# First batch row of a threshold attention + MLP-mixer kernel: three score slots in one PSUM tile, another rate of weight conversion, and the square on ScalarE

## Chip, cores, metric

One Trainium2 chip, one core. The metric is device time in microseconds (us) of one execution. Each kernel was executed several times; an execution is called a run here. The profile of the kernel before was taken on a further execution.

## The reference, cut

```python
# q, k, v: (8, 8, 576, 64) float32; tau = 0.02
scores = (q @ k^T) / 8
scores = where(scores >= rowmax(scores) - tau, scores, -1e9)
attn = softmax(scores)
x = (attn @ v), heads side by side          # (8, 576, 512)
# MLP mixer, weights in float64:
h = relu(x^T @ w_tok1) @ w_tok2             # 576 -> 256 -> 576, along the tokens
u = x + h^T
out = u + relu(u @ w_ch1) @ w_ch2           # 512 -> 1536 -> 512, along the channels
```

## The kernel before

The eight batch entries ("batch rows") are worked on in 144 units, 18 per row; a unit is 128 query rows of two heads. A unit's scores are computed at step u, its maximum, threshold and exponential in the same step, its transposes and products with v two or more steps later. From row 1 on, the MLP matmuls of the row before are strewn between the units by a quota (`fill`). The float64 weights are turned into float32 on the chip, in 31 pieces of three steps each; these 93 steps are spread over the units of rows 0 and 1 (`weight`), and a step that an MLP matmul needs is pulled forward (`need`).

The kernel uses eight PSUM banks. Two tiles of two banks hold scores, two banks hold transposes and products with v, two hold MLP results.

```python
ps_sc = ctx.enter_context(tc.tile_pool(name="ps_sc", bufs=2, space=bass.MemoryType.PSUM))
ps_tr = ctx.enter_context(tc.tile_pool(name="ps_tr", bufs=2, space=bass.MemoryType.PSUM))
ps_mm = ctx.enter_context(tc.tile_pool(name="ps_mm", bufs=2, space=bass.MemoryType.PSUM))
ctx.enter_context(tc.manual_schedule())
# ... cut ...
def f64_to_f32(dst, raw, rows, n):                         # one piece, three steps
    # ... cut: lo, hi = the two 32-bit words; a, h2 = scratch, h2 has ONE buffer ...
    nc.scalar.activation(out=lo.bitcast(I32), in_=lo, func=AF.Copy, scale=2.0**-29)
    nc.gpsimd.tensor_tensor(out=h2, in0=hi.bitcast(F32), in1=hi.bitcast(F32), op=ALU.mult)
    yield nc.vector.tensor_scalar(out=a, in0=hi, ...)      # shift, mask
    yield nc.vector.scalar_tensor_tensor(out=a, in0=hi, ...)   # OR: sign
    nc.vector.scalar_tensor_tensor(out=af, in0=h2, scalar=2.0**-30, in1=af, op0=ALU.is_ge, op1=ALU.mult)
    nc.gpsimd.tensor_tensor(out=dst..., in0=a..., in1=lo..., op=ALU.add)
# ... cut ...
def scores(u):
    b, p0, t = units[u]
    sc = [ps_sc.tile([P, 2, MAIN], F32, tag="sc", name=f"sc{h}_{u}") for h in range(2)]
    # ... cut ...
    for f in range(2):
        for n, cols, rows in parts:
            qT, kT = heads[n]
            for h in range(2):
                r = slice(D * h, D * h + D)
                nc.tensor.matmul(sc[h][rows, f, 0:HS], lhsT=qT[r, cols], rhs=kT[r, HS * f : HS * f + HS], start=True, stop=True)
    # ... cut ...
        nc.vector.tensor_reduce(out=mx[:, c], in_=sc[h][:, :, 0:HS], axis=AX.XY, op=ALU.max)
        nc.gpsimd.tensor_scalar(out=bias[:, c], in0=mx[:, c], ...)
def weigh(u):
    # ... cut ...
        nc.scalar.activation(out=eh, in_=sc[h][:, :, 0:HS], func=AF.Prelu, bias=bias[:, h : h + 1], ...)   # last reader of sc
    # ... cut: Exp in place ...
# ... cut; of the channel MLP:
def ch1(j):
    need(7 + j)
    ps = ps_mm.tile([P, GR], F32, tag="mm", name=f"c1_{b}_{i}_{j}")[:, 0:n]
    for c in range(NCC):
        nc.tensor.matmul(ps, lhsT=wc1[:, j, c, :], rhs=uT[:, c, GR * i : GR * i + n], start=(c == 0), stop=(c == NCC - 1))
    nc.scalar.activation(out=s["g"][:, j, 0:n], in_=ps, func=AF.Relu)
# ... cut; the main loop, per unit:
    scores(u)                       # if any are left
    norm(u - 1)                     # then transposes of unit u - 2
    if b_now: fill(0.4)
    weight(2)
    weigh(u)
    if b_now: fill(0.3)
    # ... products with v that are due ...
    if b_now: fill(0.3)
    weight(1 if b_now == 0 else 3)
```

## Time and profile before

| | before |
|---|---|
| time, median of 3 runs | 1425.71 us (1424.91 to 1426.79) |
| granted TensorE clock, mean | 0.982 |
| first maximum of unit 0 / 18 / 26 / 36 / 143 | 10.7 / 122.0 / 198.9 / 287.4 / 1222.0 us |
| row 0 (unit 0 to 18) | 111.3 us |
| stretch in which the conversion ends (unit 18 to 26) | 76.9 us |
| unit 26 to 143 | 1023.1 us |

The third row is read from the starts of VectorE's `tensor_reduce` in the trace. First the list of waits over the whole run (waiter, releaser: us in total, times, longest):

```profile
DVE mx L286 <- PE sc L281: 490.1, 125, 10.4
...
ACT g L447 <- PE c L446: 361.6, 160, 27.8
```

These are waits of engines that have less to do than TensorE, each for its own data: the maximum for its scores, the relu for its sum. They cost nothing by themselves.

### The profile page before, as it was taken

Reading aid. Unit: us, or ns where it says so; the run is one execution under the profiler, and the core shown is the slowest. Engines: PE = TensorE matmul, PEld = TensorE weight load, DVE = VectorE, ACT = ScalarE, POOL = GpSimd, SP = SyncE. Lnnn points to the kernel's source line nnn. Section 1 sums busy time; section 2 is a strip of 40 time slices with the busy share of each in tenths; the row PEclk is TensorE's granted clock in tenths of the full one; section 3 lists DMA queues with packets and bytes.
Section 4 is the critical chain, followed back from the end, with each engine's and each line's share of the span. In section 5 each row is a group of like instructions: output and inputs, shape, how many; then the busy total and the mean of one; then the engine's idle time right before and its main releaser. Section 6 shows DMA issues by size and latency. Waiting matters only on the chain.

```text
span 1425.1 us, 19472 instructions
## 1 busy us (share of the span) xinstructions
PE 1350.8 (95%) x6866; PEld 833.5 (58%) x6866; DVE 584.2 (41%) x1000; ACT 575.5 (40%) x1306; POOL 380.9 (27%) x712
## 2 busy tenths in 40 slices
PE   5866899978999999999999999999999999999998
PEld 3543475644756466565656566566657466566675
DVE  5778764344444443434433444434333444201000
ACT  4665453443544444353334444443333444220110
POOL 4777652221222222222212222222121222100000
PEclk9898899989999999999999999999999999999999
DMA  5444544443444434433343434443433433300000
GB/s 123 118 110 126 142 124 98 95 116 81 96 120 112 108 84 109 107 93 79 95 99 77 120 83 111 99 102 72 103 84 85 110 89 80 81 17 15 8 8 23
DMA packets 257376, 128.34 MB, mean 90 GB/s; under 512 B 208064, under 2 KB 221376, under 8 KB 257280
## 3 DMA queue, kind: packets, MB, share of 16 engines
q1 hardware_dynamic: 134000, 111.75, 30.0%
q10 hardware_dynamic: 123280, 15.35, 6.8%
q8 instruction: 55, 0.90, 0.3%
q14 instruction: 41, 0.34, 0.1%
HBM read 43.25 MB, written 9.44 MB: 37 GB/s over the span
## 4 chain that ended last, share of the span: by engine, by line
PE 82%; DVE 5%; SPq 4%; POOL 3%; ACT 2%; DMA 2%; issue 1%; DVEq 0%; POOLq 0%
PE c L462 26%; PE c L446 24%; PE sc L281 10%; PE pv L388 7%; PE t L417 4%; SPq L353 4%; PE t L424 3%; PE pv L383 2%; DVE T L343 2%; PE tx L407 1%; DVE mx L286 1%; PE c L458 1%; DMA eT<-T 1%; PE tr L332 1%; POOL scratch L156 1%
## 5 line engine op out<-in xcount | busy, mean ns | idle before, releaser
L446 PE MATMUL c<-xT,wc 128*128 128x256 f32 (+1 forms) x1920 | 405.5, 363 | 1.3 <-DVE xT L428 0.8
L286 DVE TENSOR_REDUCE mx<-sc 128x1 f32<-128x576 f32 x288 | 204.5, 751 | 490.1 <-PE sc L281 490.1
L462 PE MATMUL c<-wc,g 128*128 128x512 f32 x864 | 389.5, 597 | 0.0
L446 PEld LDWEIGHTS c<-xT,wc 128*128 128x128 f32 x1920 | 331.1, 190 | 74.7 <-issue 29.5
L287 POOL TENSOR_SCALAR bias<-mx,toff 128x1 f32<-128x1 f32 x288 | 76.0, 265 | 795.0 <-DVE mx L286 744.1
L296 ACT ACTIVATE e<-sc,bias 128x576 f32<-128x576 f32 x288 | 198.6, 738 | 179.0 <-POOL bias L287 167.2
L462 PEld LDWEIGHTS c<-wc,g 128*128 128x128 f32 x864 | 157.6, 190 | 177.3 <-issue 176.1
L447 ACT ACTIVATE g<-c 128x256 f32<-128x256 f32 (+1 forms) x240 | 86.8, 362 | 391.1 <-PE c L446 361.6
L299 ACT ACTIVATE e<-e,ntau 128x576 f32<-128x576 f32 x288 | 220.2, 773 | 0.0
L281 PE MATMUL sc<-kT,qT 64*128 64x288 f32 (+1 forms) x1280 | 197.4, 442 | 23.7 <-ACT e L296 15.1
L309 POOL TENSOR_SCALAR e<-e,rr 128x576 f32<-128x576 f32 x288 | 213.5, 754 | 16.3 <-DVE rr L306 4.0
L343 DVE STREAM_TRANSPOSE T<-e 128x1152 f32<-128x1152 f32 x126 | 172.5, 1369 | 17.2 <-DMA eT<-T 12.7
L281 PEld LDWEIGHTS sc<-kT,qT 64*128 64x128 f32 (+1 forms) x1280 | 107.1, 182 | 108.2 <-issue 49.5
L388 PE MATMUL pv<-eT,lv 128*64 128x256 f32 x1024 | 128.6, 396 | 0.0
L467 DVE COPY o<-c 128x512 f32<-128x512 f32 x36 | 24.6, 684 | 192.3 <-PE c L462 192.3
L388 PEld LDWEIGHTS pv<-eT,lv 128*64 128x64 f32 x1024 | 77.5, 143 | 39.9 <-issue 4.9
L424 PE MATMUL t<-w,a 128*128 128x288 f32 x256 | 76.1, 426 | 11.6 <-DVE xT L428 9.8
L417 PE MATMUL t<-x,w 128*128 128x512 f32 (+1 forms) x160 | 77.2, 621 | 0.0
L393 ACT COPY xT<-pv 128x256 f32<-128x256 f32 x64 | 23.8, 372 | 113.6 <-PE pv L388 113.3
L428 DVE TENSOR_TENSOR xT<-xT,t 128x288 f32<-128x288 f32 x64 | 27.9, 441 | 95.8 <-PE t L424 95.7
L424 PEld LDWEIGHTS t<-w,a 128*128 128x128 f32 x256 | 45.4, 191 | 35.3 <-DVE xT L428 14.7
L299 ACT ACTIVATION_READ_ACCUMULATOR e<-e,ntau 128x1 f32 x288 | 57.1, 198 | 0.0
(43 smaller groups left out, 621.8 us busy)
## 6 DMA issues: line engine op xcount, KB each, us to landing
eT<-T SPq DMA_DIRECT2D x896, 72.0 KB, 2.1
scratch<-in_moe_w_ch_dram SPq DMA_DIRECT2D x24, 512.0 KB, 3.7
lv<-in_v_dram SPq DMA_DIRECT2D x32, 288.0 KB, 3.4
out_dram<-o SPq DMA_DIRECT2D x36, 256.0 KB, 2.1
eT<-T SPq DMA_DIRECT2D x224, 36.0 KB, 1.9
lq<-in_q_dram ACTq DMA_DIRECT2D x104, 72.0 KB, 2.2
lk<-in_k_dram ACTq DMA_DIRECT2D x104, 72.0 KB, 2.7
lq<-in_q_dram SPq DMA_DIRECT2D x24, 72.0 KB, 3.4
```

Source lines behind the costliest of these rows:

```text
L281: nc.tensor.matmul(sc[h][rows, f, 0:HS], lhsT=qT[r, cols], rhs=kT[r, HS * f : HS * f + HS], start=True, stop=True)
L286: nc.vector.tensor_reduce(out=mx[:, c], in_=sc[h][:, :, 0:HS], axis=AX.XY, op=ALU.max)
L296: nc.scalar.activation(out=eh, in_=sc[h][:, :, 0:HS], func=AF.Prelu, bias=bias[:, h : h + 1], scale=SCALE, alpha=STEEP)
L299: nc.scalar.activation(out=eh, in_=eh, func=AF.Exp, bias=ntau, accum_out=rs[:, h : h + 1])
L309: nc.gpsimd.tensor_scalar(out=eh, in0=eh, scalar1=rr[:, h : h + 1], scalar2=1.0, op0=ALU.mult, op1=ALU.mult)
L343: nc.vector.transpose(out=T.rearrange("p (a c n x) -> p c a n x", a=4, c=NK, n=n)[:, :, :, place, :], in_=e.rearrange("p (c a x) -> p c a ...
L388: nc.tensor.matmul(to[r], lhsT=lv[:, j, :], rhs=eT[:, j], start=False, stop=(c == NI - 1), skip_group_check=True)
L417: nc.tensor.matmul(ps, lhsT=w1[0:M, t, P * m : P * m + P], rhs=s["x"][0:M, t, :], start=(t == 0), stop=(t == NT - 1))
L424: nc.tensor.matmul(ps, lhsT=s["a"][:, m, P * c : P * c + P], rhs=w2[:, m, HS * f : HS * f + HS], start=(m == 0), stop=(m == NTK - 1))
L446: nc.tensor.matmul(ps, lhsT=wc1[:, j, c, :], rhs=uT[:, c, GR * i : GR * i + n], start=(c == 0), stop=(c == NCC - 1))
L447: nc.scalar.activation(out=s["g"][:, j, 0:n], in_=ps, func=AF.Relu)
L462: nc.tensor.matmul(flat, lhsT=s["g"][:, j, P * t : P * t + P], rhs=wc2[:, j, :], start=False, stop=(j == NJ - 1), skip_group_check=True)
```

## The change

Intent: give row 0, where no engine is full, a third score slot, by using in row 0 the two banks that the MLP needs only from row 1 on; do fewer conversion steps in row 0 and more in row 1 (three a unit become two, five become seven); take the square off GpSimd; share the middle transposes' copies between ScalarE and VectorE; load the first q and k from two queues. To let two banks serve both purposes, the six banks become one tile, of which slices are handed out. The core of the diff:

```diff
-    ps_sc = ctx.enter_context(tc.tile_pool(name="ps_sc", bufs=2, space=bass.MemoryType.PSUM))
+    ps_big = ctx.enter_context(tc.tile_pool(name="ps_big", bufs=1, space=bass.MemoryType.PSUM))
     ps_tr = ...
-    ps_mm = ctx.enter_context(tc.tile_pool(name="ps_mm", bufs=2, space=bass.MemoryType.PSUM))
+    banks = ps_big.tile([P, 6, MAIN], F32, name="banks")
+    mm_last, mm_held = [0], [None]
+    def mm_bank(hold=False):
+        i = mm_last[0] ^ 1
+        if i == mm_held[0]:
+            i ^= 1
+        mm_last[0] = i
+        if hold:
+            mm_held[0] = i
+        return banks[:, 4 + i, :]
@@ f64_to_f32
-        nc.gpsimd.tensor_tensor(out=h2, in0=hi.bitcast(F32), in1=hi.bitcast(F32), op=ALU.mult)
+        nc.scalar.activation(out=h2, in_=hi.bitcast(F32), func=AF.Square)
@@ first loads of q and k
-    load_qk(0, nc.sync)
+    load_qk(0, (nc.sync, nc.scalar))
@@ scores
-        sc = [ps_sc.tile([P, 2, MAIN], F32, tag="sc", name=f"sc{h}_{u}") for h in range(2)]
+        at = [h if b else (2 * u + h) % 3 for h in range(2)]
+        sc = [banks[:, 2 * a : 2 * a + 2, 0:HS] for a in at]
-        for f in range(2): ... for n, cols, rows in parts: ... for h in range(2): ...
+        order = [(f, part, h) for f in range(2) for part in parts for h in range(2)]
+        for f, (n, cols, rows), h in order if b else sorted(order, key=lambda o: o[2]):
@@ turn
-        on = nc.scalar.copy if third == 1 else nc.vector.tensor_copy
+        on = nc.scalar.copy if third == 1 and u % 2 else nc.vector.tensor_copy
@@ tok1, tok2, ch1, ch2: ps_mm.tile(...) becomes mm_bank(); ch2 holds its bank until its last part
@@ main loop
-        weight(2)
+        weight(4 if b_now else 1)
-        weight(1 if b_now == 0 else 3)
+        weight(3 if b_now else 1)
```

More of the change, by code (lines that the diff above doesn't have):

```diff
@@ L100, in load_qk @@
             h, c = divmod(i, 2)
-            for src, t in zip((q, k), loaded[n]):
-                eng.dma_start(
+            for src, t, on in zip((q, k), loaded[n], eng):
+                on.dma_start(
                     out=t[32 * i : 32 * i + 32], in_=src[b, 2 * p + h, :, 32 * c : 32 * c + 32].rearrange("(n t) d -> t n d", t=32)
@@ L224 @@
     load_piece(0)
-    load_qk(1, nc.sync)
+    load_qk(1, (nc.sync, nc.sync))
     load_v(0)
@@ L275, in scores @@
             parts = [(b * NP + p0 + i, slice(P * c, P * c + P), slice(0, P))]
-        for f in range(2):
-            for n, cols, rows in parts:
-                qT, kT = heads[n]
-                for h in range(2):
-                    r = slice(D * h, D * h + D)
-                    nc.tensor.matmul(sc[h][rows, f, 0:HS], lhsT=qT[r, cols], rhs=kT[r, HS * f : HS * f + HS], start=True, stop=True)
+        order = [(f, part, h) for f in range(2) for part in parts for h in range(2)]
+        for f, (n, cols, rows), h in order if b else sorted(order, key=lambda o: o[2]):
+            r = slice(D * h, D * h + D)
+            qT, kT = heads[n]
+            nc.tensor.matmul(sc[h][rows, f, :], lhsT=qT[r, cols], rhs=kT[r, HS * f : HS * f + HS], start=True, stop=True)
         mx = small.tile([P, 2], F32, tag="mx", name=f"mx_{u}")
@@ L285, in scores @@
             c = slice(h, h + 1)
-            nc.vector.tensor_reduce(out=mx[:, c], in_=sc[h][:, :, 0:HS], axis=AX.XY, op=ALU.max)
+            nc.vector.tensor_reduce(out=mx[:, c], in_=sc[h], axis=AX.XY, op=ALU.max)
             nc.gpsimd.tensor_scalar(out=bias[:, c], in0=mx[:, c], scalar1=toff, scalar2=-SCALE, op0=ALU.add, op1=ALU.mult)
@@ L295, in weigh @@
             eh = e[:, S * h : S * h + S].rearrange("p (f x) -> p f x", f=2)
-            nc.scalar.activation(out=eh, in_=sc[h][:, :, 0:HS], func=AF.Prelu, bias=bias[:, h : h + 1], scale=SCALE, alpha=STEEP)
+            nc.scalar.activation(out=eh, in_=sc[h], func=AF.Prelu, bias=bias[:, h : h + 1], scale=SCALE, alpha=STEEP)
         for h in range(2):
@@ L413, in tok1 @@
                 s["a"] = work.tile([P, NTK, DM], F32, tag="a", bufs=1, name=f"a_{b}")
-            ps = ps_mm.tile([P, DM], F32, tag="mm", name=f"t1_{b}_{m}")
+            ps = mm_bank()
             for t in range(NT):
@@ L421, in tok2 @@
             need(6)
-            ps = ps_mm.tile([P, HS], F32, tag="mm", name=f"t2_{b}_{c}_{f}")
+            ps = mm_bank()[:, 0:HS]
             for m in range(NTK):
@@ L443, in ch1 @@
                 s["g"] = work.tile([P, NJ, GR], F32, tag="g", bufs=1, name=f"g_{b}_{i}")
-            ps = ps_mm.tile([P, GR], F32, tag="mm", name=f"c1_{b}_{i}_{j}")[:, 0:n]
+            ps = mm_bank()[:, 0:n]
             for c in range(NCC):
@@ L452, in ch2 @@
             if part == 0:
-                s["ps"] = ps_mm.tile([P, NCC, P], F32, tag="mm", name=f"c2_{b}_{i}_{t}")
+                s["ps"] = mm_bank(hold=True).rearrange("q (c d) -> q c d", c=NCC)
             ps = s["ps"]
@@ L465, in ch2 @@
             if part == 3:
+                mm_held[0] = None
                 o = work.tile([P, DM], F32, tag="o", name=f"o_{b}_{i}_{t}")
@@ L551 @@
             if t < 8 and m < len(pairs):
-                load_qk(m, nc.scalar if b_now else nc.sync, t % 4)
+                load_qk(m, (nc.scalar if b_now else nc.sync,) * 2, t % 4)
                 if t % 4 == 3:
```

## The prediction

> **What bounds the kernel now.** I read the page first: over the whole span TensorE is the bound.
>
> ```profile
> PE 1350.8 (95%) x6866; PEld 833.5 (58%) x6866; DVE 584.2 (41%) x1000; ACT 575.5 (40%) x1306; POOL 380.9 (27%) x712
> PE   5866899978999999999999999999999999999998
> DVE  5778764344444443434433444434333444201000
> ```
>
> The reader sees that TensorE is at 9 in nearly every slice except the first ten or so. The change touches only the beginning, so I then asked for busy time by stretch. The cuts are the first score matmul (8.4), the first maximum of batch row 1, which is unit 18 (122.0), and the end of the weight conversion (199).
>
> ```profile
> 8.40:122.00 113.60, 84.63 (x518) 51.80 (x518) 84.80 (x164) 70.98 (x153) 79.85 (x113) 0.92 0.49 119
> 122.00:199.00 77.00, 61.98 (x304) 39.02 (x305) 60.92 (x95) 38.98 (x82) 52.31 (x63) 0.90 0.50 135
> 199.00:1425.00 1226.00, 1204.15 (x6045) 742.70 (x6044) 436.27 (x737) 464.29 (x1071) 247.43 (x527) 0.99 0.35 84
> ```
>
> Columns: stretch, length, then busy time of PE, weight load, VectorE, ScalarE, GpSimd, then clock, DMA share, GB/s. Batch row 0 (18 units in 113.6 us) has no engine above 75%: it runs on a loop of waits. After 199 us, TensorE idles 22 us of 1226, so what row 0 gains arrives at the end one for one, and nothing else can. The ceiling on what a perfect row 0 could give is small against 1425.
>
> The waits of 8 to 123 us show the loop.
>
> ```profile
> ACT eT L334 <- PE tr L332: 24.5, 17, 2.3
> PEld sc L281 <- ACT e L296: 18.5, 18, 4.2
> DVE scratch L163 <- POOL scratch L156: 14.7, 15, 1.5
> PE sc L281 <- ACT e L296: 11.9, 8, 3.3
> DVE mx L286 <- PE sc L281: 9.1, 9, 2.4
> ```
>
> Columns: waiter, releaser, total us, times, longest. Three things to see. The next unit's scores wait for Prelu of this unit, because two score buffers hold exactly one unit; Prelu stands in ScalarE's queue behind the copy of the middle transposes, which waits for TensorE: a ring of 5.9 us per unit in the first 45 us. VectorE waits 14.7 us for the square on GpSimd. Later in row 0 the period is 5.7 us in units without value matmuls and 6.3 to 7.6 with them; the mean is (122.0 - 10.7)/18 = 6.18 us.
>
> **What the Trainium skill says.**
> "ScalarE: Activation LUTs", section "What ACT_TABLE_LOAD costs": an ACTIVATE with immediates takes 186 ns + 0.833 ns per element, the same for every function; a switch of table set costs 1283 ns plus a drain. The trace agrees: the conversion's existing Copy of 128x512 takes 683 ns in row 0 (the formula gives 613; its source has a stride), and the one table load took 1283 ns. The section "Table sets" says cheap functions are in every set; it names relu, copy, identity and abs, not Square, so that Square needs no load is my assumption. No run shows it yet.
> "GPSIMD Engine Reference", section "Key points": GpSimd shares its SBUF interfaces with VectorE, in contention with VectorE instructions that have two SBUF inputs. The trace agrees: the two-input OR of the conversion (128x512) took 0.69 us alone, 1.10 us on average in row 0, and 1.66 at worst.
> "TensorE: Matmul & The Clock Gate", section "The mechanism": matmuls in different row groups overlap. The trace agrees: at 107.67 and 107.68 us the matmuls of the two heads start together, and the eight records of a unit end within 1.24 us though each lasts 0.40. The same page, section "What's actually happening", has an idle TensorE at half clock; here a score record lasts 0.68 us in the cold stretches and 0.40 in the warm ones.
>
> **The change part by part.**
>
> *Start.* The first q and k tiles are issued from two queues. Eight issues at about 0.53 us each on one queue (0.73 to 5.0 us) become four on each, behind the tau load on ScalarE's. The last issue moves from 4.5 to about 2.8 to 3.2 us, the first transposes and score matmul (8.41) follow. Estimate: **-1.7 us**.
>
> *Three score slots.* In row 0 head h of unit u waits for the Prelu three heads back, not two, so TensorE need not wait for Prelu of the unit just before. The 18.5 us wait and the ring above go.
>
> *Scores head by head.* Sorting by head puts matmuls of one row group one after the other. Starts in one row group are 0.24 us apart in the warm state, so eight take about 8 x 0.24 + 0.2 = 2.1 us instead of 1.24; the first head is ready after about 1.1 us, as before, and the second by the time VectorE has done the first maximum (0.75 us). So it costs TensorE 0.9 us a unit, and little latency.
>
> *Conversion steps.* 18 units x 3 steps = 54 steps (18 pieces) become 36 (12 pieces). VectorE loses 6 pieces x (0.46 + 1.10 + 0.69) = 13.5 us. The square moves to ScalarE: GpSimd loses 1.4 us a piece, ScalarE gains about 0.65, and VectorE's 14.7 us of waiting goes, since the square now comes a step or more ahead of its use.
>
> *Copies.* Nine of 18 middle copies go from ScalarE to VectorE, 9 x 0.54 = 4.9 us.
>
> Load per unit of row 0 after:
> - VectorE: two maxima 1.42 (back to back), norm 0.45, copies 2.5 x 0.5 = 1.27, conversion 2/3 x 2.0 = 1.34, transposes of q and k 0.34: **4.8 us** (before, 4.7 busy and 1.6 waiting).
> - ScalarE: Prelu and Exp 3.3, half a copy 0.24, conversion 2/3 x 1.33 = 0.9, value copies 0.25: **4.7 us**.
> - TensorE, warm: scores 2.1, transposes 1.3, values 1.34 on average: **4.7 us**, and more when cold.
> - GpSimd: bias 0.53, norm 1.5, conversion 0.85, the rest 0.15: 3.0 us, from 4.4.
>
> Three engines at 4.7 to 4.8 us cannot interleave perfectly. In the units with four large value groups per nine, the ring is: maxima 1.42, norm 0.45, first eT copy 0.54 (it frees a transpose bank), value matmuls 2.55, first head's scores 1.1, and in half of them the last transposes 0.65 before the values: 6.1 to 6.7, mean 6.4 us. The four units without values run at VectorE's 4.8; the one with small value groups at about 5. Mean (4 x 6.4 + 4 x 4.8 + 5)/9 = 5.5 us, against 6.18: 18 x 0.65 = **-11.5 us**. I take off 1.5 us for the first five units, where TensorE is cold and serial scores double in length too: **-10 us**.
>
> *Row 1.* 57 steps (19 pieces) are left for row 1 instead of 39 (13), at 7 per unit instead of 5, so conversion still ends in its ninth unit, and no later step is pulled forward. VectorE in these units: before 60.9 busy and some 8 waiting for GpSimd, of 77.0. After: 6 more pieces x 2.1 = +12.6, less contention with GpSimd on the other 13, about -4, the 7.2 us of waiting gone: about 70 of 77, so the stretch is close to VectorE-bound. ScalarE gets 19 squares (+12.4) and 6 copies (+4.1), about 56 busy. Its square now waits in order for VectorE to have used the previous one (one buffer), with Prelu behind it. Estimate: **+1 us**, with a wide spread (-3 to +8).
>
> *After row 1.* The matmuls, buffers (two banks, one skipped while held) and quotas are as before: 0.
>
> Sum: -1.7 - 10 + 1 = -10.7, so **1415.0 us**.
>
> **The rivals.**
> *A. Row 0 becomes engine-bound and nothing else.* If the three slots decouple the engines well, row 0 runs at 4.9 us a unit: 18 x 1.28 = -23, with the start -25: about 1401. For it: three loads are equal at 4.8. Against it: the order on each queue is fixed, TensorE has value matmuls in front of the next scores, and two transpose banks remain.
> *B. The gain is given back in row 1.* VectorE and ScalarE together have 29 us more in the 77 us where they already stalled TensorE (15 us idle there). If Prelu behind the squares holds up the scores and the relus that free the two MLP banks, 1 us a unit more is lost: 1421 to 1424. For it: the old trace has up to 5.6 us of ScalarE waiting for bias in that stretch. Against it: the removed GpSimd square was itself a cause.
> *C. Serial scores on a cold TensorE eat the gain.* At half clock, scores take about 4.1 us and transposes 2.4, 6.5 us a unit, no better than 6.18. If half of row 0 is cold, the row saves about 5 us: 1420. For it: 10 us stretches at half clock are seen in the old row 0 (the slice at 60 to 70 us has 0.55). Against it: a busier TensorE should be cold less.
> *D. Square needs its own table.* Then two loads per piece, 31 x 2 x 1.28 = 80 us on ScalarE, and the time goes above 1460. It is unlikely.
>
> **Range and chances.** B and C together give about 1424, A gives 1401; the range is 1402 to 1424. Faster by 2% means below 1397.2, more than rival A gives: 0.03. Slower by 2% needs D: 0.02. Within 2%: 0.95.
>
> **What would show each step.** In the profile after: first score matmul near 6.7 us; unit 18's first maximum near 110 us (122.0 before), that is 5.6 us a unit; no wait of VectorE's last conversion step on GpSimd; score records in row 0 of one head after the other, 2.1 us per unit when warm; no further table load; conversion ending about 77 us after unit 18; TensorE's idle time after that near 22 us as before. I would be wrong if row 0 takes under 92 or over 108 us for its 18 units, if the stretch from unit 18 to the end of conversion grows by more than 8 us, or if anything after it differs by more than 3 us.

## More of the kernel before

TensorE's timeline somewhere in the middle (start, length, line, count):

```profile
240.30 1.20 PE L281 MATMUL sc<-kT,qT 64*64 64x288 f32 x16
241.43 7.17 PE L446 MATMUL c<-xT,wc 128*128 128x256 f32 x32
248.53 1.24 PE L281 MATMUL sc<-kT,qT 64*128 64x288 f32 x8
```

Scores, 32 MLP records (four groups of eight) and the next unit's scores follow each other with no gap.

Second, the view of one source line, for the channel MLP's first matmuls, each of which leaves two records (their duration min/median/max in ns, then what ended TensorE's and its weight loader's idle time before them: us, times):

```profile
L446 PE MATMUL c<-xT,wc x1920: 272/379/483, 177.7 to 1410.2; 128*128 128x256 f32 x156, 128*128 128x128 f32 x36
...
  issue: 29.5, 79
...
  ACT g L447: 3.0, 7
```

TensorE hardly ever waits for anyone before these 1920 records.

## The result

| | before | after |
|---|---|---|
| time, median (4 runs each) | 1425.31 us (1424.25 to 1426.79) | 2076.61 us (2069.09 to 2077.3) |
| ratio, 95% interval | | 1.4556 [1.452, 1.4593] |
| granted TensorE clock | 0.982 | 0.932 |
| first maximum of unit 0 / 18 / 26 / 36 / 143 | 10.7 / 122.0 / 198.9 / 287.4 / 1222.0 | 9.6 / 106.6 / 237.5 / 367.9 / 1810.4 |
| row 0 | 111.3 | 97.0 |
| unit 18 to 26 | 76.9 | 130.9 |
| unit 26 to 143 | 1023.1 | 1572.9 |

The kernel became 45% slower. A ratio, here and below, is the mean time of one kernel's fast runs over that of the other's fast runs of the same rounds, so it is not quite the ratio of the medians.

Row 0, which the change is about, became 14.3 us shorter. The loss lies behind it: 54.0 us in units 18 to 26, 549.8 us in units 26 to 143, and another 53.6 us after unit 143's maximum, where only MLP work and the last units' rest are left (256.6 us against 203.1). In the last two the change touches nothing but the PSUM tile and the way its banks are handed out. The page of the kernel after, the lines that answer to those of before, and the clock:

```profile
PE 1506.6 (73%) x6866; PEld 862.5 (42%) x6866; DVE 588.7 (28%) x1009; ACT 592.2 (29%) x1328; POOL 346.6 (17%) x681
...
PE   5756677777777677777676766677777776688888
...
DVE  5874422322323222212222322222312222210000
...
PEclk9976999879999799989999989998999998999999
```

Not one slice of TensorE is at 9 any more; most stand at 6 or 7, and VectorE has fallen from 3 or 4 to 2. No engine took over as the bound: all idle more. The stretches (length, then busy time of PE, PEld, DVE, ACT, POOL, then clock, DMA share, GB/s), cut at the first maxima of units 18 and 26:

```profile
7.20:106.60 99.40, 70.60 (x514) 44.51 (x515) 72.78 (x155) 69.30 (x151) 52.97 (x89) 0.97 0.45 103
106.60:237.50 130.90, 79.86 (x306) 44.83 (x304) 73.98 (x113) 53.31 (x107) 43.79 (x55) 0.75 0.38 105
237.50:2067.00 1829.50, 1356.16 (x6048) 773.13 (x6048) 439.78 (x737) 468.36 (x1071) 248.57 (x527) 0.94 0.24 56
```

In the last stretch TensorE does 6048 records as before (6045 were recorded), but idles 1829.5 - 1356.2 = 473 us instead of 22. Its busy time also grew by 152 us; its granted clock there is 0.94 instead of 0.99, which can be no more than part of this (1204 us scaled by 0.99/0.94 gives an estimate of 64 us), and the rest was not taken apart. VectorE, ScalarE and GpSimd are busy for the same time within 1%. So the work is the same and its overlap is lost. The waits say between whom (same columns as before; lines of the whole run and, last, the view of line L460, the channel MLP's first matmul, L446 of before):

```profile
DVE mx L300 <- PE banks L295: 874.2, 129, 14.4
ACT g L461 <- PE banks L460: 716.5, 236, 34.6
...
ACT e L310 <- PE banks L476: 216.4, 35, 9.6
```

```profile
L460 PE MATMUL banks<-xT,wc x1920: 274/379/796, 199.0 to 2051.5; 128*128 128x256 f32 x156, 128*128 128x128 f32 x36
...
  DVE mx L300: 187.2, 106
  ACT e L310: 179.6, 90
  ACT g L461: 98.9, 160
```

The first and second are old waits grown. The third is new, and it has no reason in the data: L310 is Prelu, which reads scores in banks 0 to 3; L476 is the channel MLP's second matmul, which writes bank 4 or 5. The view of L460 shows the opposite direction: a matmul that writes bank 4 or 5 waits for the maximum (L300) and for Prelu, which read banks 0 to 3. (These sums and counts take TensorE's and its weight loader's idle time together, so they must not be added to the 473 us. With the filter `--engine PE` TensorE alone waits 53 times, 81.9 us, for the maximum and 44 times, 80.1 us, for Prelu.) The timeline shows how it looks where before 32 records ran without a gap; the bracket is the idle time ahead and what ended it:

```profile
307.31 1.99 PE L460 MATMUL banks<-xT,wc 128*128 128x256 f32 x8 [1.74 <-ACT e L310]
309.78 1.99 PE L460 MATMUL banks<-xT,wc 128*128 128x256 f32 x8 [0.47 <-ACT g L461]
312.25 1.00 PE L295 MATMUL banks<-kT,qT 64*128 64x288 f32 x6 [0.47 <-ACT g L461]
```

Two MLP banks alternate, and yet the second group of eight waits for the relu (L461) of the group just before, in the other bank; the first waits for Prelu. The last row waits, for scores in banks 0 to 3, for a relu of bank 4 or 5. Row 0 has the same waits. TensorE's first 20 us:

```profile
7.22 2.30 PE L295 MATMUL banks<-kT,qT 64*128 64x288 f32 x8 [7.22 <-DVE kT L278]
12.54 2.30 PE L295 MATMUL banks<-kT,qT 64*128 64x288 f32 x8 [3.03 <-ACT e L310]
18.13 2.30 PE L295 MATMUL banks<-kT,qT 64*128 64x288 f32 x8 [3.29 <-ACT e L310]
```

Unit 1's head 0 goes to slot (2*1+0) mod 3 = 2, that is banks 4 and 5, which nobody has used yet. It waits 3.03 us for unit 0's Prelu all the same.

### The profile page after: what moved, and what is told of

It reads as the page before. It is cut to its first block, busy times and chain, and to the rows that moved or that the text cites. A ratio compares the mean times of both kernels' runs of the same rounds, so it can differ in the third digit from the quotient of the medians.

```text
span 2067.0 us, 19772 instructions
## 1 busy us (share of the span) xinstructions
PE 1506.6 (73%) x6866; PEld 862.5 (42%) x6866; DVE 588.7 (28%) x1009; ACT 592.2 (29%) x1328; POOL 346.6 (17%) x681
## 4 chain that ended last, share of the span: by engine, by line
PE 68%; DVE 15%; ACT 12%; issue 3%; SPq 1%; DMA 1%; DVEq 0%; ACTq 0%; POOL 0%
PE banks L460 23%; PE banks L476 20%; DVE mx L300 10%; PE banks L295 8%; ACT e L310 7%; PE pv L402 5%; PE banks L438 4%; PE banks L431 4%; ACT g L461 4%; PE pv L397 2%; DVE xT L442 1%; PE banks L472 1%; DVE o L482 1%; DVE T L357 1%; SPq L367 1%
## 5 line engine op out<-in xcount | busy, mean ns | idle before, releaser
L460 PE MATMUL banks<-xT,wc 128*128 128x256 f32 (+1 forms) x1920 | 474.8, 394 | 219.4 <-DVE mx L300 81.9
L460 PEld LDWEIGHTS banks<-xT,wc 128*128 128x128 f32 x1920 | 347.9, 205 | 356.8 <-DVE mx L300 105.3
L476 PE MATMUL banks<-wc,g 128*128 128x512 f32 x864 | 415.8, 625 | 100.6 <-ACT e L310 53.5
L300 DVE TENSOR_REDUCE mx<-banks 128x1 f32<-128x576 f32 x288 | 204.7, 752 | 874.3 <-PE banks L295 874.2
L310 ACT ACTIVATE e<-banks,bias 128x576 f32<-128x576 f32 x288 | 197.2, 738 | 397.8 <-PE banks L476 216.4
L461 ACT ACTIVATE g<-banks 128x256 f32<-128x256 f32 (+1 forms) x240 | 87.1, 363 | 716.7 <-PE banks L460 716.5
L476 PEld LDWEIGHTS banks<-wc,g 128*128 128x128 f32 x864 | 162.0, 198 | 304.6 <-issue 163.0
L295 PE MATMUL banks<-kT,qT 64*128 64x288 f32 (+1 forms) x1280 | 187.6, 444 | 74.3 <-ACT g L461 24.1
L295 PEld LDWEIGHTS banks<-kT,qT 64*128 64x128 f32 (+1 forms) x1280 | 101.0, 183 | 160.8 <-ACT g L461 43.3
L438 PE MATMUL banks<-w,a 128*128 128x288 f32 x256 | 104.2, 542 | 67.2 <-ACT e L310 32.8
```

Source lines behind the costliest of these rows:

```text
L295: nc.tensor.matmul(sc[h][rows, f, :], lhsT=qT[r, cols], rhs=kT[r, HS * f : HS * f + HS], start=True, stop=True)
L300: nc.vector.tensor_reduce(out=mx[:, c], in_=sc[h], axis=AX.XY, op=ALU.max)
L310: nc.scalar.activation(out=eh, in_=sc[h], func=AF.Prelu, bias=bias[:, h : h + 1], scale=SCALE, alpha=STEEP)
L438: nc.tensor.matmul(ps, lhsT=s["a"][:, m, P * c : P * c + P], rhs=w2[:, m, HS * f : HS * f + HS], start=(m == 0), stop=(m == NTK - 1))
L476: nc.tensor.matmul(flat, lhsT=s["g"][:, j, P * t : P * t + P], rhs=wc2[:, j, :], start=False, stop=(j == NJ - 1), skip_group_check=True)
```

## The experiments

**Theory 1**: the framework that builds the program orders accesses by tile, not by slice. With one tile, every write waits for the last readers of any bank, and every reader for the last write of any bank. The packed traces, which keep each instruction's semaphore waits, support it: with one tile, unit 1's first weight load carries a wait, the one that Prelu ended in the view above; in e4_fixed, with separate tiles (run below), it carries none, and unit 1's first matmul starts at 9.30 us, directly behind unit 0's. **Rival 1**: seven conversion steps a unit in row 1 upset the later schedule. **Rival 2**: the way `mm_bank` chooses banks (one held, one used again at once) is at fault.

### e1_one_tile_only: the kernel before, with the one tile and nothing else of the change

```diff
-    ps_sc, ps_mm = pools of two tiles each
+    ps_big ...; banks = ps_big.tile([P, 6, MAIN], F32, name="banks"); mm_bank() as in the change
-        sc = [ps_sc.tile([P, 2, MAIN], F32, tag="sc", name=f"sc{h}_{u}") for h in range(2)]
+        sc = [banks[:, 2 * h : 2 * h + 2, :] for h in range(2)]
-            ps = ps_mm.tile(...)          # tok1, tok2, ch1, ch2
+            ps = mm_bank()...
```

> The kernel before with one edit: its score buffers and MLP banks become slices of one PSUM tile, each at a bank of its own; conversion steps, the square on GpSimd, copies, loads and the order of the scores stay as before. Theory (the tile framework orders every access to one tile, whichever bank it touches, so each matmul into it waits for the last reader of any bank, and each reader for the last matmul): 2040 to 2110 us, as slow as the change. Rival 1 (the extra conversion steps and squares of row 1 upset the row and all that follow): 1425. Rival 2 (the bank choice with one bank held starves the MLP matmuls): also about 2070, but then score matmuls would not wait for readers of MLP banks.

Measured: 2074.54 us (2073.55 to 2075.55), ratio 1.455 [1.4531, 1.4569]. The view of the channel MLP's first matmul:

```profile
L458 PE MATMUL banks<-xT,wc x1920: 275/379/796, 202.1 to 2056.1; 128*128 128x256 f32 x156, 128*128 128x128 f32 x36
...
  DVE mx L298: 187.2, 106
  ACT e L308: 174.5, 90
```

The same waits, almost to the number (after: 187.2 and 179.6). The tile, with `mm_bank`, makes the whole loss, with the old conversion rates, the old square and the old order of scores. Rival 1 falls. Rival 2 stands so far, for `mm_bank` came with the tile.

### e2_old_psum: the change, with PSUM and scores as before

```diff
-    banks = ps_big.tile([P, 6, MAIN], F32, name="banks")   # and mm_bank
+    ps_sc, ps_mm = pools of two tiles each; scores' order as before
```

> The change without its PSUM part: two score buffers and two MLP banks from pools as before, scores in the old order; the conversion steps, the square on ScalarE, the copies and the split first load as in the change. Theory of the one tile: 1408 to 1422, since batch row 0 of the changed kernel already took 97 us for its 18 units against 111. Rival 1 (conversion steps in row 1 are to blame): about 2000 or more.

Measured: 1421.82 us (1420.15 to 1424.62), ratio 0.9975 [0.9962, 0.9988]. Everything in the change but the tile, the slots and the order of the scores is worth a quarter of a per cent.

### e3_three_tiles: the change, with three tiles of two banks

```diff
-    banks = ps_big.tile([P, 6, MAIN], F32, name="banks")
+    slots = [ps_big.tile([P, 2, MAIN], F32, tag=f"slot{i}", name=f"slot{i}") for i in range(3)]
-        return banks[:, 4 + i, :]
+        return slots[2][:, i, :]
-        sc = [banks[:, 2 * a : 2 * a + 2, 0:HS] for a in at]
+        sc = [slots[a][:, :, 0:HS] for a in at]
```

> The change with the six banks as three tiles of two banks: two score slots, and a third whose two banks serve as third score slot in row 0 and as the two MLP banks later. Theory of the one tile: score and MLP matmuls no longer wait for each other, but each MLP matmul still waits for the reader of the other MLP bank: between the two, estimated 1600 to 1750 from 0.5 to 0.9 us lost at some 460 groups of MLP matmuls. Rival 2 (bank choice): stays near 2070. If the framework orders by bank and something else is at work: stays near 2070 too.

The banks, their order and `mm_bank` are those of the change; only the borders of the tiles differ. Measured: 1650.72 us (1649.19 to 1653.86), ratio 1.1574 [1.1557, 1.1591]. The view of the same matmul:

```profile
L460 PE MATMUL slot<-xT,wc x1920: 274/379/797, 180.2 to 1636.3; 128*128 128x256 f32 x156, 128*128 128x128 f32 x36
...
  ACT g L461: 178.8, 239
  DVE xT L442: 74.0, 60
```

The waits for maximum and Prelu, now other tiles, are gone. Those for relu and for the addition, which read the other bank of the same tile, remain and have grown. This is what theory 1 says and rival 2 does not: the choice of banks is unchanged, and 426 us went. Two banks in one tile still cost 1650.72 - 1418.94 = 232 us against the next run. That run drops `mm_bank` too, but its choice of banks can hardly be what costs: a replay of the kernel's own scheduling code, without the chip, gives the bank that was given last again in only 6 of 356 cases, while TensorE alone (with `--engine PE`) waits 115 times for the relu.

### e4_fixed: the change, with a tile for every buffer

Slots 0 and 1 are tiles of their own; slot 2 comes from a pool that is closed after row 0, and two MLP tiles are then opened in its place.

```diff
+    row0 = ExitStack()
+    ps_x = row0.enter_context(tc.tile_pool(name="ps_x", bufs=1, space=bass.MemoryType.PSUM))
+    mm_pool = []
+    def mm_bank():
+        return mm_pool[0].tile([P, MAIN], F32, tag="mm", name="mm")
+    def slot(a, h, u):
+        pool = ps_x if a == 2 else ps_sc
+        return pool.tile([P, 2, MAIN], F32, tag=f"sc{a}", name=f"sc{h}_{u}")[:, :, 0:HS]
@@ main loop, after weigh(u)
+        if u == UB - 1:
+            row0.close()
+            mm_pool.append(ctx.enter_context(tc.tile_pool(name="ps_mm", bufs=2, space=bass.MemoryType.PSUM)))
```

> The whole change as it was meant: three score slots of row 0 as tiles of their own, the third from a pool that is closed after row 0, then two MLP banks from a pool of two as before. Theory: 1400 to 1418, below the kernel with the old PSUM pools, because TensorE can start the next unit's first head before this unit's Prelu. My prediction's own sum, which assumed separate banks, says 1415. If the three slots are worth nothing, it equals the kernel with the old PSUM pools.

Measured: 1418.94 us (1417.47 to 1421.67), ratio 0.9954 [0.9942, 0.9965]. The change as it was meant is 0.5% faster than the kernel before. The view of the matmul is back where it was. TensorE's first 24 records, three units' scores, are done within 9.46 us, where the one tile had the third unit only begin at 18.13 us:

```profile
L457 PE MATMUL mm<-xT,wc x1920: 272/379/796, 168.3 to 1401.1; 128*128 128x256 f32 x156, 128*128 128x128 f32 x36
...
  issue: 29.9, 80
  ACT g L458: 5.7, 10
```

```profile
7.21 9.46 PE L292 MATMUL sc<-kT,qT 64*128 64x288 f32 x24 [7.21 <-DVE kT L275]
```

Its stretches, cut at its own units 18 and 26:

```profile
7.20:99.90 92.70, 72.99 (x518) 46.16 (x518) 72.70 (x155) 69.75 (x151) 52.34 (x89) 0.98 0.49 110
99.90:195.00 95.10, 70.82 (x305) 44.08 (x306) 71.99 (x113) 52.16 (x106) 43.00 (x55) 0.82 0.52 146
```

With this the 651 us are settled. What is left is a second question: row 0 is 21.0 us shorter than before (90.3 against 111.3), but units 18 to 26 are 18.2 us longer (95.1 against 76.9). **Why is the gain given back?** In that stretch the trace of e4_fixed has these waits, among others (waiter, releaser: us in total, times, longest):

```profile
ACT scratch L167 <- DVE scratch L174: 15.4, 6, 4.6
ACT scratch L166 <- DMA scratch<-in_moe_w_ch_dram: 11.4, 4, 6.6
...
PE mm L435 <- DVE xT L439: 10.7, 2, 7.5
```

L166 and L167 are the conversion's Copy and Square, L174 its last VectorE step, L435 and L439 the token MLP's second matmul and the addition that empties its bank. **Theory A**: the raw weights arrive late, because their loads queue behind the sixteen transfers of each block turn on the same queue. **Theory B**: seven steps a unit are too many for the engines that must also serve TensorE, wherever the weights are. The next four runs are e4_fixed with one thing altered.

### e5_loads_on_gpsimd_queue: raw weights from another queue

```diff
-        nc.sync.dma_start(out=like(raw, dst), in_=src)
+        nc.gpsimd.dma_start(out=like(raw, dst), in_=src)
```

> The mended change (e4) with the loads of the raw weights issued from GpSimd's queue instead of SyncE's. In e4 unit 18 came 22 us earlier than before, but unit 26 only 4 us earlier. Theory A (the raw loads of row 1 stand behind blocks of sixteen eT transfers on SyncE's queue, 10 us each, and VectorE, ScalarE and TensorE wait for them): the wait of the conversion for DMA goes, unit 26 comes 10 to 16 us earlier than before, 1403 to 1412. Theory B (VectorE and ScalarE are simply full in row 1): same as e4, 1417 to 1420.

Measured: 1422.05 us (1419.18 to 1426.71), ratio 0.997 [0.9953, 0.9988]. ScalarE's wait for the transfers shrank from 11.4 to 1.4 us, and VectorE's (7.7 us in e4_fixed) is gone, yet the stretch takes 92.0 us instead of 95.1, and the other two waits are still there:

```profile
ACT scratch L167 <- DVE scratch L174: 19.8, 9, 4.5
...
PE mm L435 <- DVE xT L439: 7.9, 2, 5.2
```

By this run theory A explains about 3 of the 18 us. It is not a clean limit: the loads are now issued by GpSimd, which is idle for 5.0 us in this stretch just before them. The whole did not gain, since the first maximum came at 15.2 us instead of 9.5: the weights' first loads now run beside those of q and k.

### e6_three_steps: the old rates, three and five

```diff
-        weight(4 if b_now else 1)
+        weight(2)
```

> The mended change with the conversion rates of before: three steps a unit in row 0, five in row 1; slots, square on ScalarE, copies as in the change. Theory A and B alike: row 0 slower than in e4 (5.4 to 5.8 us a unit against 5.0), the stretch from unit 18 to 26 no longer than the 77 us of before: 1412 to 1420. If fewer steps in row 0 are what row 0's gain comes from, its 18 units take 105 us or more.

Measured: 1411.49 us (1409.6 to 1415.48), ratio 0.9898 [0.9884, 0.9912].

```profile
8.40:114.20 105.80, 79.97 (x518) 50.04 (x518) 85.43 (x173) 76.79 (x163) 59.97 (x95) 0.92 0.51 125
114.20:188.50 74.30, 63.37 (x301) 38.30 (x302) 57.99 (x96) 45.94 (x94) 36.70 (x50) 0.91 0.52 140
```

Row 0 takes 102.3 us, 12.0 more than in e4_fixed, but units 18 to 26 take 74.2, less even than before. The kernel without this part of the change is the better one, by 7 us.

### e7_five_in_row1: two steps in row 0, five in row 1

```diff
-        weight(4 if b_now else 1)
+        weight(2 if b_now else 1)
```

> The mended change with two steps a unit in row 0 and five instead of seven in row 1, so that conversion ends some four units later. Theory A (loads behind the eT blocks): fewer pieces per block of eT transfers, so less waiting: unit 26 comes 8 to 14 us earlier than before, 1405 to 1414. Theory B (full engines) gives the same sign, but needs no change in the waits for DMA. If the loss is only moved to units 26 to 31: 1417 to 1421.

Measured: 1415.52 us (1413.56 to 1415.7), ratio 0.9918 [0.9905, 0.9931]. Row 0 takes 90.4 us and units 18 to 26 take 78.1: with five steps, the stretch is short again, although row 0 did as little as in e4_fixed. With e5_loads_on_gpsimd_queue, which changed the loads and not the rate, this supports theory B: it is mainly the rate. But 18 fewer steps were done in row 0, and they come due. A stretch behind unit 26 in this kernel, where in e6_three_steps TensorE is busy for 20.50 of 20.50 us:

```profile
198.50:219.00 20.50, 13.98 (x45) 5.66 (x46) 9.86 (x14) 5.41 (x11) 6.06 (x7) 0.67 0.38 92
```

TensorE is idle for 6.5 us here. Its timeline names the wait (6.95 us, of which 5.1 lie in this stretch):

```profile
203.64 2.08 PE L473 MATMUL mm<-wc,g 128*128 128x512 f32 x2 [6.95 <-POOL wc L175]
```

The channel MLP's second matmuls (L473) pull the remaining steps forward and wait for their last one, GpSimd's addition (L175). The steps have to be paid for somewhere; of the rates tried, three and five did it at the least cost.

### e8_square_on_gpsimd: the square back on GpSimd

```diff
-        nc.scalar.activation(out=h2, in_=hi.bitcast(F32), func=AF.Square)
+        nc.gpsimd.tensor_tensor(out=h2, in0=hi.bitcast(F32), in1=hi.bitcast(F32), op=ALU.mult)
```

> The mended change with the square back on GpSimd. If the move of the square was worth something in row 0 (my prediction: VectorE's 14.7 us of waiting for it), unit 18 comes 3 to 10 us later than in e4; if the square on ScalarE holds up Prelu in row 1 (part of rival B), the stretch from unit 18 to 26 is shorter than e4's 95 us. Together 1414 to 1424.

Measured: 1421.82 us (1419.18 to 1424.21), ratio 0.9963 [0.995, 0.9976], against 0.9954 of e4_fixed. Row 0 91.1 us against 90.3, units 18 to 26 97.4 against 95.1. At these rates the square is worth little, and Square behind VectorE's last step on one buffer is not what makes the stretch long, for without it the stretch is no shorter.

The third question is where the 1% of e6_three_steps comes from.

### e9_slots_only: the kernel before, with three slots and scores head by head

```diff
+    slot(), mm_bank(), row0.close() as in e4_fixed
-        for f in range(2): ... for h in range(2): ...
+        order as in the change
```

> The kernel before with three score slots in row 0 (tiles of their own, as in e4) and the scores head by head, and nothing else of the change. If the slots are what row 0 gains from at three steps a unit: units 0 to 18 in 103 to 106 us (e6 took 102, before 111) and 1413 to 1419. If the square and the copies carry it: 109 to 111 us and 1424 to 1428.

Measured: 1425.75 us (1423.87 to 1427.11), ratio 0.9999 [0.9986, 1.0013]; row 0 111.1 us against 111.3. The third slot, with the scores head by head, gives nothing at all. In row 0 VectorE still waits 17 times, 17.5 us in all, for the square on GpSimd.

### e10_e6_old_copies: e6_three_steps, all middle copies on ScalarE

```diff
-        on = nc.scalar.copy if third == 1 and u % 2 else nc.vector.tensor_copy
+        on = nc.scalar.copy if third == 1 else nc.vector.tensor_copy
```

> e6 (three slots, old conversion rates, square on ScalarE) with all middle copies on ScalarE as before. My prediction had the nine copies moved to VectorE as a cost to VectorE of 4.9 us, not as a gain: if so, 1 to 4 us faster than e6, 1408 to 1411. If the copies free the ring of the middle transposes, slower than e6 by 2 to 5 us.

Measured: 1411.78 us (1408.97 to 1413.73), ratio 0.9896 [0.9882, 0.991]. No difference in the whole; row 0 was 99.4 us against 102.3. Sharing the copies brings nothing; whether it costs 2.9 us in row 0 stays open, since each is one profile and the totals are equal.

### e11_e6_square_gpsimd: e6_three_steps, square on GpSimd

```diff
-        nc.scalar.activation(out=h2, in_=hi.bitcast(F32), func=AF.Square)
+        nc.gpsimd.tensor_tensor(out=h2, in0=hi.bitcast(F32), in1=hi.bitcast(F32), op=ALU.mult)
```

> e6 with the square back on GpSimd. If VectorE's wait for the square (14.7 us in row 0 of before) is worth something at three steps a unit, unit 18 comes 4 to 10 us later than in e6 and the time is 1414 to 1422; with two steps a unit (e8 against e4) it was worth about 1 us in row 0 and 2.6 us in all.

Measured: 1430.34 us (1426.62 to 1430.88), ratio 1.002 [1.0007, 1.0033]; row 0 115.1 us. Without the square, slots, split start and shared copies together are slightly slower than the kernel before; why row 0 grew by 3.8 us stays open.

### e12_e6_one_two: e6_three_steps, its three steps of row 0 parted one and two

```diff
-        weight(2)
+        weight(2 if b_now else 1)
-        weight(3 if b_now else 1)
+        weight(3 if b_now else 2)
```

> e6 with the three steps of row 0 as one before weigh and two after it, instead of two and one. If conversion in front of Prelu on ScalarE's queue holds up row 0, it is 1 to 4 us faster than e6, 1407 to 1411; if the order within the unit does not matter, the same as e6.

Measured: 1413.21 us (1410.73 to 1414.39), ratio 0.9905 [0.9892, 0.9919]; row 0 100.8 us. The place of the steps within the unit does not matter measurably.

### e13_square_only: the kernel before, with the square on ScalarE

```diff
-        nc.gpsimd.tensor_tensor(out=h2, in0=hi.bitcast(F32), in1=hi.bitcast(F32), op=ALU.mult)
+        nc.scalar.activation(out=h2, in_=hi.bitcast(F32), func=AF.Square)
```

> The kernel before with the square on ScalarE and nothing else. Slots alone gave nothing (e9), and without the square the slots and copies gave nothing (e11); slots with the square gave 1.0 per cent (e10). If the square alone is the gain: 1411 to 1415, unit 18 at 111 to 115 us. If it needs the three slots, because ScalarE's longer queue otherwise holds up the next scores: 1418 to 1425, unit 18 at 117 us or later.

Measured: 1419.72 us (1417.67 to 1421.87), ratio 0.9952 [0.9939, 0.9964]; row 0 107.1 us. The four corners, each as a ratio to the kernel before, all at three and five steps:

| | old slots and order | three slots, head by head |
|---|---|---|
| square on GpSimd | 1 | 0.9999 (e9_slots_only) |
| square on ScalarE | 0.9952 (e13_square_only) | 0.9896 (e10_e6_old_copies, which has the split start too) |

The third slot, with what came with it, is worth half a per cent once the square has left GpSimd, and nothing before. One line of code (the square) gives as much as the whole mended change.

The versions beside each other, times in us from the first maxima:

| | time | row 0 | unit 18 to 26 | unit 26 to 143 |
|---|---|---|---|---|
| before | 1425.3 | 111.3 | 76.9 | 1023.1 |
| after | 2076.6 | 97.0 | 130.9 | 1572.9 |
| e1_one_tile_only | 2074.5 | 112.8 | 114.0 | 1577.3 |
| e2_old_psum | 1421.8 | 92.9 | 95.1 | 1018.6 |
| e3_three_tiles | 1650.7 | 90.5 | 109.8 | 1188.0 |
| e4_fixed | 1418.9 | 90.3 | 95.1 | 1017.9 |
| e5_loads_on_gpsimd_queue | 1422.1 | 89.9 | 92.0 | 1017.6 |
| e6_three_steps | 1411.5 | 102.3 | 74.2 | 1022.2 |
| e7_five_in_row1 | 1415.5 | 90.4 | 78.1 | 1030.8 |

The table leaves out the time before the first maximum and that after unit 143's. The latter took 203.0 to 203.1 us in all of these but three: 256.6 us in the kernel after, 257.0 in e1_one_tile_only and 252.1 in e3_three_tiles, again the kernels with banks that share a tile. Some expectations were missed: e4_fixed and e6_three_steps lie 1 us or less outside theirs, e5_loads_on_gpsimd_queue, e7_five_in_row1 and e10_e6_old_copies outside every range named, and e11_e6_square_gpsimd 8 us above.

The best versions that ran are e6_three_steps and e10_e6_old_copies, 1% below the kernel before.

## Why the prediction was wrong

It said 1415 us, within 2%; the kernel took 2076.61, and nothing in its range or its rivals comes near.

- **The step that failed** is "After row 1": "The matmuls, buffers (two banks, one skipped while held) and quotas are as before: 0." The matmuls and quotas were. The buffers were not: what had been four tiles was one, and a wait is made per tile. The term of 0 measured 549.8 us in units 26 to 143 and 53.6 us after them. The same error is in "Three score slots" ("head h of unit u waits for the Prelu three heads back"): in the kernel after, it waits for the last Prelu of any slot, as unit 1's first wait of 3.03 us shows, so row 0 took 97.0 us where the same program with separate tiles took 90.3. The prediction read the diff as a map of banks and did not ask who makes the waits, and from what. e1_one_tile_only isolates this cause, e3_three_tiles shows it in part, e4_fixed takes it away.
- **The sum without this error** is tested by e4_fixed: 1415.0 predicted, 1418.94 measured. The total is near by luck: two terms are off and cancel.
- **Row 0**, -10 us, was -21.0: a unit took 90.3/18 = 5.0 us, not 5.5. Rival A (4.9 us a unit) was nearly right in size. Its reason, that row 0 becomes bound by its engines, is not shown: VectorE and TensorE, the busiest, are busy for 73 of 92.7 us there.
- **Row 1**, +1 us (-3 to +8), was +18.2. This is rival B at a larger size. It was mis-sized because the prediction counted busy time and found 70 of 77 us on VectorE; VectorE was indeed busy for 72.0 us, but of 95.1. e6_three_steps and e7_five_in_row1 show that the rate of seven is the cause, e5_loads_on_gpsimd_queue that late weights are about a sixth of it, e8_square_on_gpsimd that the square on ScalarE is not. Seen in the trace, but isolated by no run, is the way: the addition that frees an MLP bank (L439) comes on VectorE's queue behind conversion steps, and TensorE waits up to 7.5 us for it. In this longest case late weights took part: of the 7.5 us VectorE itself waited 3.7 for raw weights.

```profile
150.59 0.43 DVE L168 TENSOR_SCALAR scratch<-scratch 128x512 uint32<-128x512 uint32 x1 [3.67 <-DMA scratch<-in_moe_w_ch_dram]
151.05 0.69 DVE L171 SCALAR_TENSOR_TENSOR scratch<-scratch 128x512 uint32<-128x512 uint32 x1
...
151.66 0.81 DVE L439 TENSOR_TENSOR xT<-xT,mm 128x288 f32<-128x288 f32 x2
...
152.16 3.73 PE L435 MATMUL mm<-w,a 128*128 128x288 f32 x8 [7.54 <-DVE xT L439]
```

- **Start**, -1.7 us: not shown. The first score matmul came at 7.22 us instead of 8.41 (-1.2), and the first maximum at 9.6 instead of 10.7. But over all kernels with the split load, one profile each, the first score matmul lies between 7.2 and 9.6 us (mean of ten 8.6, without e5_loads_on_gpsimd_queue), and over the four without it between 8.1 and 8.4 (mean 8.2).
- **Scores head by head**, +0.9 us of TensorE a unit: wrong, it was 0. In row 0 of the kernel after, warm, eight records of a unit take as long as before (1.24 us then):

```profile
74.42 1.25 PE L295 MATMUL banks<-kT,qT 64*128 64x288 f32 x8
```

  They still start in pairs 0.02 us or less apart (74.42 and 74.43, 74.77 and 74.78), as before (107.65 and 107.66; the prediction read 107.67 and 107.68). With it rival C falls. The packed traces show why. The record that ends a head's scores carries a signal when the head has a tile of its own; in e4_fixed these are the seventh and the eighth record of a unit (starts 63.03 and 63.04), so each pair is one record of either head. And in e9_slots_only a unit's head 1 had to wait for its slot: its first record started at 72.61 us, ahead of head 0's fourth at 72.73. The matmuls of one row group did not hold back those of the other, though the program has all of one head first; the prediction took them to run one after the other.
- **Conversion steps**: in row 0 the wait of VectorE for the square is gone, as predicted. In row 1 it is not: in e4_fixed VectorE waits 8.3 us in 3 waits for the square on ScalarE, as against 7.2 us in 7 for GpSimd's before, which the prediction counted as gone. Two steps instead of three in row 0 are worth 12.0 us there (90.3 against 102.3), and this is what is given back. "Less contention with GpSimd, about -4" hardly came: the OR's 31 instructions took 33.8 us before, 33.0 after and 32.1 in e4_fixed, all over both rows, though their median fell from 1115 to 825 ns. An OR of 128x512 took 0.67 to 0.69 us where GpSimd was idle, mostly about 1.1 in row 0 of before, beside the norm and the square on GpSimd, and 1.66 wherever it ran beside GpSimd's addition; of row 1's ORs, 10 of 19 ran beside the addition in e4_fixed, 5 of 13 before.
- **Copies**, +4.9 us of VectorE: no effect on the total (e6_three_steps against e10_e6_old_copies).
- **Rival D** falls: one table load in the whole kernel after, 1283 ns, before any conversion; Square's 31 instructions took 628 ns on average, Copy's 635.

Of the checks that the prediction named, two gave the alarm at once: units 18 to 26 grew by 54 us, not under 8, and what followed differed by hundreds of us, not under 3.

## What to carry to other kernels

Before you merge buffers into one tile, ask at which grain the waits are made: here slices of one tile counted as one buffer, and cost 45%; a pool that is closed and opened again shares the same banks without this. When waits appear between instructions that touch different banks, look for a common tile and test it alone on the old kernel. And work that is moved out of a stretch has to be placed somewhere: look at the stretch that receives it by the order on its queues, for its busy share (about 70 of 77 us was predicted) can look bearable while it holds up the engine that sets the end.

## What the Trainium skill lacked or had wrong

- "Perfetto Trace Analysis", section "Matmuls", advises that independent groups of matmuls rotate through different PSUM banks, so that emptying one overlaps the next. No run speaks against it, but it lacks that rotation in the program is not enough: e1_one_tile_only rotates through the same banks as the kernel before and takes 2074.5 instead of 1426.0 us, because they are one tile. No page says at which grain waits on a tile are made.
- "ScalarE: Activation LUTs", section "Table sets", names relu, copy, identity and abs as in every set, not Square. In the kernel after, Square among Prelu, Exp, Relu and Copy needed no load beyond the first (one of 1283 ns, 31 Squares).
- "TensorE: Matmul & The Clock Gate", section "The mechanism", has matmuls in different row groups overlap, and has all matmuls start and end in the order of the program. The order of the starts differs here: with the records of one head given ahead of those of the other, the two heads' records start in pairs 0.02 us or less apart, eight took 1.25 us, as with the heads in turn (1.24 us), and in e9_slots_only head 1's first record started at 72.61 us, before head 0's fourth at 72.73.
